# A recurrence and a two-layer network on one core: scans instead of triangle sums for four chunks, a third set of input buffers, a longer search for the order

## The chip, the cores and the metric

The kernel runs on one core of a Trainium2 chip. Its time is the device time of the whole program in microseconds (us); the figure for a kernel is the median of its runs. A core has TensorE (PE, matmuls), VectorE (DVE), ScalarE (ACT), GpSimd (POOL) and SyncE (SP), which issues the transfers here. Each engine works through its own list of instructions in order and waits on semaphores for the others.

## The reference

Two parts follow each other. The first is a gated recurrence over 768 time steps for each of 4 batches and 8 heads, with a 48 by 48 state; the second is a two-layer network over all 3072 tokens.

```python
f = 1.0 / (1.0 + np.exp(-f_logit))                 # (4, 8, 768, 48)
for t in range(S):
    state = f[:, :, t, :, None] * state + np.einsum('bhd,bhe->bhde', k[:, :, t], v[:, :, t])
    y[:, :, t] = np.einsum('bhd,bhde->bhe', q[:, :, t], state)
x = y.transpose(0, 2, 1, 3).reshape(B * S, H * D)  # 3072 tokens x 384
h = x @ w_in                                       # 384 -> 2048
sp = np.where(h > 20.0, h, np.log1p(np.exp(np.minimum(h, 20.0))))
g = h * np.tanh(sp)
out = g @ w_out                                    # 2048 -> 384
```

All is float32, and the result has to be close to it, which is why each matrix operand of the network is split into a high and a low part and three products are taken of each pair.

## The kernel before

**The recurrence** is cut into 24 chunks: 6 stretches of 128 steps for each of 4 batches, in the order stretch, then batch. Heads are worked on in pairs, four pairs to a chunk. A chunk goes through these steps. `load` brings the gate logits l, k, q (128 x 512 each) and v. `prep` takes the logarithm of the gate (ACT) and sums it along the chunk: for the first `NS` = 8 chunks by matmuls with an upper triangle (PE, line 362; these chunks are loaded transposed, as `ft`), for the others by a scan on DVE (line 367). Two exponentials of the sums (ACT) scale k and q; for chunks 1 to 7 k is scaled on POOL, else on DVE. `attn0` multiplies q and k in halves of 64 steps (scores, line 398) and masks them (DVE). `attn1` transposes k (line 423, copied by ACT to kt). `attn2` forms the state's update (line 440), sums it in mid and tmp (DVE, for the first four chunks partly ACT). `attn3` adds up the outputs (lines 474 and 486), decays the state (POOL), and writes the high and low parts of the outputs into xt; after a few chunks three transfers of SP rearrange rows of xt (line 525, the swap).

**The network** works on groups of 512 tokens (four chunks), 6 groups, and 16 tiles of the hidden width: 96 units. A unit is nine matmuls for the hidden tile (`moe_in`, line 219), a chain of nine steps for the activation (`mish`, lines 229 to 237: ACT, ACT, DVE, DVE, ACT, ACT, DVE, ACT, POOL), and, two units later, nine matmuls into the three output banks (`moe_out`, line 242). Groups 0 and 1 take turns with the first eight and the last eight tiles, so the weights are needed little by little. Each of the 16 weight tiles is loaded as 64-bit numbers (line 320) and split into high and low parts by `split_w` (two ACT and four DVE instructions, lines 322 to 330).

**The order.** No loop issues an instruction directly. Each step is recorded with its engine, an assumed cost and what it reads and writes; `Plan.order` then packs all steps in time by ranks, forwards and backwards, ten times for each of five settings, keeps the packing with the earliest end, and `issue` emits the steps in that order on every engine's list. `port` marks steps of DVE that must not overlap POOL in the plan. Where the plan leaves PE a gap before the first output of the network, `issue` puts in fillers, matmuls of zeros (`idle`, line 310):

```python
if self.start[i] <= self.start[self.until]:
    while at + 313.0 < self.start[i]:
        self.idle()
        at += 213.0 if at > 6500.0 else 426.0
```

The inputs l, k, q and v have two buffers each, so chunk n reuses those of chunk n - 2 (`i = n % 2`); kt, inv, mid and tmp have one each, and the two halves of the masked scores a one each.

**The end.** The fast path holds only where no decay has become too small. After all units DVE counts the chunks' final decays that are large enough, PE adds the counts, DVE writes the `flag` (lines 620 to 625); every engine loads it into a register (line 633), and where the count is short a general, slow path is run (line 634 on). With these inputs it is jumped over.

## Time and profile before

| | |
|---|---|
| median of 3 runs | 529.99 us (527.87 to 534.02) |
| profiled execution, its own time | 533.71 us |
| its span, first to last instruction | 531.9 us |
| mean granted TensorE clock | 0.990 of full speed |
| instructions | 13034 |
| idle fillers on PE | 66 matmuls, 132 records, 20.7 us busy |
| moved by DMA | 48.91 MB, 92 GB/s on average |

An instruction of PE appears as a weight load (PEld) and a matmul (PE); float32 matmuls have two records each. In rows of groups stand line, engine, operation, tiles and shapes, count, then busy us and mean ns of one, then the idle time of the engine just before them and what ended it. In the chain of waits each row has start, length, engine and line: followed back from the end, it names at each step what the step had waited for. An engine's name with a q (SPq, PEldq) is its sequencer: branches, semaphores, issues of transfers.

### The profile page before, as it was taken

The numbers are of one execution on the slowest core, as the hardware profiler recorded it, in microseconds if no ns is written. First come the engines' busy times: TensorE is split into PE (matmuls) and PEld (weight loads), VectorE is DVE, ScalarE is ACT, GpSimd is POOL, SyncE is SP. The second block draws the span as 40 slices with busy tenths as digits, with TensorE's granted clock in tenths as the row PEclk, the third lists the DMA queues.
The fourth block names the chain that finished last, engine by engine and source line by source line (L and its number), as shares of the span: only waits on it lengthen the run. The fifth ranks groups of instructions, "written<-read, shape, count | busy, mean of one in ns | idle before, by whom it ended". The sixth has DMA issues, their size and how long they took to land.

```text
span 531.9 us, 13034 instructions
## 1 busy us (share of the span) xinstructions
PE 512.8 (96%) x5358; PEld 409.7 (77%) x5358; DVE 369.7 (70%) x588; ACT 415.4 (78%) x731; POOL 157.4 (30%) x134
## 2 busy tenths in 40 slices
PE   8899999999899999999999999999999999999993
PEld 7678777777677777787787777787787787778882
DVE  4478999899897887866576777567657563645451
ACT  6777988888789798878778788878878776778770
POOL 2231442334132322412322332413131222132320
PEclk9899999999899999999999999999999999999998
DMA  7597554344230443321212330112221000000001
GB/s 263 208 293 257 167 173 131 88 154 140 98 99 21 143 138 110 118 64 60 62 41 90 101 100 25 58 41 90 61 79 41 4 0 33 26 33 1 1 1 67
DMA packets 22629, 48.91 MB, mean 92 GB/s; under 512 B 2656, under 2 KB 3808, under 8 KB 22560
## 3 DMA queue, kind: packets, MB, share of 16 engines
q1 hardware_dynamic: 22560, 47.98, 28.1%
q8 instruction: 44, 0.72, 0.6%
q14 instruction: 25, 0.20, 0.1%
HBM read 39.32 MB, written 6.29 MB: 86 GB/s over the span
## 4 chain that ended last, share of the span: by engine, by line
PE 82%; DVE 7%; DMA 3%; ACT 3%; issue 2%; SPq 0%; POOL 0%; DVEq 0%; ACTq 0%
PE h L219 35%; PE o L242 34%; PE at L486 2%; PE at L474 2%; PE at L440 2%; DMA xt<-xt 2%; PE at L423 2%; PE at L398 2%; DVE wt L325 1%; DMA raw<-ww 1%; DVE g L232 1%; DVE wl L330 1%; DVE n L231 1%; PE at L362 1%; PE o L310 1%
## 5 line engine op out<-in xcount | busy, mean ns | idle before, releaser
L237 POOL TENSOR_TENSOR gl<-g,gh 128x512 fp32r<-128x512 f32 x96 | 129.9, 1356 | 302.5 <-ACT gh L236 274.3
L219 PE MATMUL h<-xt,wh 128*128 128x512 f32 x576 | 185.9, 404 | 3.4 <-DVE g L235 2.4
L219 PEld LDWEIGHTS h<-xt,wh 128*128 128x128 f32 x576 | 105.7, 189 | 31.1 <-DVE g L235 4.8
L242 PE MATMUL o<-gh,wh 128*128 128x512 f32 x288 | 116.5, 405 | 0.0
L219 PE MATMUL h<-xt,wl 128*128 128x512 f32 x288 | 114.2, 397 | 0.0
L242 PE MATMUL o<-gl,wh 128*128 128x512 f32 x288 | 113.7, 395 | 0.0
L242 PE MATMUL o<-gh,wl 128*128 128x512 f32 x288 | 113.7, 395 | 0.0
L231 DVE SCALAR_TENSOR_TENSOR n<-n 128x512 f32<-128x512 f32 x96 | 71.1, 740 | 54.7 <-ACT n L230 54.5
L235 DVE TENSOR_TENSOR g<-g,h 128x512 f32<-128x512 f32 x96 | 65.3, 682 | 42.1 <-ACT h L234 41.7
L229 ACT ACTIVATE n<-h,hcap 128x512 f32<-128x512 f32 x96 | 65.7, 685 | 31.5 <-PE h L219 30.8
L233 ACT ACTIVATE h<-n,two 128x512 f32<-128x512 f32 x96 | 65.8, 686 | 29.3 <-DVE g L232 29.3
L236 ACT ACTIVATE gh<-g 128x512 fp32r<-128x512 f32 x96 | 60.1, 627 | 16.1 <-DVE g L235 14.1
L232 DVE TENSOR_TENSOR g<-h,n 128x512 f32<-128x512 f32 x96 | 66.1, 689 | 8.9 <-POOL gl L237 1.1
L230 ACT ACTIVATE n<-n,hcap 128x512 f32<-128x512 f32 x96 | 69.2, 721 | 2.1
L219 PEld LDWEIGHTS h<-xt,wl 128*128 128x128 f32 x288 | 54.4, 189 | 13.3
L242 PEld LDWEIGHTS o<-gh,wh 128*128 128x128 f32 x288 | 54.0, 188 | 13.5 <-ACT ob L588 0.3
L242 PEld LDWEIGHTS o<-gl,wh 128*128 128x128 f32 x288 | 54.0, 187 | 13.3
L242 PEld LDWEIGHTS o<-gh,wl 128*128 128x128 f32 x288 | 54.1, 188 | 11.8
L234 ACT ACTIVATE h<-h 128x512 f32<-128x512 f32 x96 | 55.9, 582 | 1.8
L519 DVE TENSOR_TENSOR xt<-at,xt 128x256 fp32r<-128x256 f32 x40 | 15.9, 418 | 13.4 <-ACT xt L512 13.2
L502 POOL TENSOR_TENSOR state<-tmp,ends 128x256 f32<-128x256 f32 x20 | 16.7, 834 | 28.6 <-PE at L474 22.1
L404 DVE TENSOR_TENSOR a<-at,causal 128x256 f32<-128x256 f32 x44 | 17.7, 418 | 7.4 <-PE at L398 7.3
(102 smaller groups left out, 525.2 us busy)
## 6 DMA issues: line engine op xcount, KB each, us to landing
raw<-ww SPq DMA_DIRECT2D x16, 768.0 KB, 5.2
v<-vn SPq DMA_DIRECT2D x24, 256.0 KB, 3.7
k<-kk SPq DMA_DIRECT2D x23, 256.0 KB, 3.1
q<-qq SPq DMA_DIRECT2D x23, 256.0 KB, 2.9
out<-ob SPq DMA_DIRECT2D x18, 256.0 KB, 2.3
l<-fl SPq DMA_DIRECT2D x16, 256.0 KB, 2.7
xt<-xt SPq DMA_DIRECT2D x15, 128.0 KB, 2.1
l<-ft SPq DMA_DIRECT2D x7, 256.0 KB, 3.8
```

The source lines that it names most:

```text
L219: nc.tensor.matmul(h, w[:, j, a * P : (a + 1) * P], xt[:, x, a, :], start=(n == 0), stop=(n == 3 * NK - 1))
L229: ("act", T_ACT(GT, True, 1), 0, lambda: nc.scalar.activation(u, h, AF.Relu, bias=hcap, scale=-1.0)),
L230: ("act", T_ACT(GT, False, 1), 0, lambda: nc.scalar.activation(u, u, AF.Exp, bias=hcap, scale=-1.0)),
L231: ("dve", T_DVE(GT), 1, lambda: nc.vector.scalar_tensor_tensor(n, u, 2.0, u, ALU.add, ALU.mult)),
L232: ("dve", T_DVE(GT), 0, lambda: nc.vector.tensor_tensor(g, h, n, ALU.mult)),
L233: ("act", T_ACT(GT, False, 1), 0, lambda: nc.scalar.activation(h, n, AF.Ln, bias=two)),
L234: ("act", T_ACT(GT, True), 0, lambda: nc.scalar.activation(h, h, AF.Exp, scale=-1.0)),
L235: ("dve", T_DVE(GT), 0, lambda: nc.vector.tensor_tensor(g, g, h, ALU.mult)),
L236: ("act", T_ACT(GT), 0, lambda: nc.scalar.activation(gh, g, AF.Copy)),
L237: ("pool", T_POOL(GT), 1, lambda: nc.gpsimd.tensor_tensor(gl, g, gh.bitcast(F32), ALU.subtract)),
L242: nc.tensor.matmul(o, w[:, j, m * P : (m + 1) * P], x, start=(first and i == 0), stop=(last and i == 2))
L404: add("dve", T_DVE(NP * CH), lambda e=e: nc.vector.tensor_tensor(a_[e], sc[e], causal[:, None, :].broadcast_to([P, NP, CH]), ALU.mult), [k ...
```

## The change

Seven edits are made together.

- `NS` is 4 instead of 8: chunks 4 to 7 are summed by scans on DVE from an untransposed load, as the later ones were. Their k stays on POOL, and inv in SBUF (`n < 2 * GC`).
- l, k, q and v have three buffers each (`NR`), kt, inv, mid and tmp two, a four.
- `Plan.order` goes on for 100 trials: the best ranks so far are disturbed by random amounts and packed again.
- A filler has 256 columns, and is put in where the plan's gap is over 527 ns.
- The count of the decays is recorded before the last two units' outputs, and DVE's last copies of outputs also wait for the flag.
- In the general path loops take the place of unrolled code, and some transfers go to ACT's queue.
- The program is built with 256 bytes of scratch for dynamic transfers.

```diff
-NS = 8
+NS = 4
...
+TRIALS = 100
+NR = 3
...
-                if best is None or end < best:
-                    best, self.start = end, start
+                if best is None or end < best[0]:
+                    best = end, rank, ahead, haste
+                    self.start = start
                 back = self.pack([-start[i] - cost[i] for i in range(count)], ahead, haste, True)
                 rank = [-back[i] - cost[i] for i in range(count)]
...
+        pick = random.Random(1)
+        for k in range(TRIALS):
+            end0, rank0, ahead, haste = best
+            spread = (200.0, 600.0, 2000.0, 6000.0)[k % 4]
+            rank = [r + pick.gauss(0.0, spread) for r in rank0]
+            start = self.pack(rank, ahead, haste)
+            end = max(start[i] + cost[i] for i in range(count))
+            if end < end0:
+                best = end, rank, ahead, haste
+                self.start = start
...
-                    while at + 313.0 < self.start[i]:
+                    while at + 527.0 < self.start[i]:
                         self.idle()
-                        at += 213.0 if at > 6500.0 else 426.0
+                        at += 427.0 if at > 6500.0 else 853.0
...
-        l_, k_, q_ = (ring(nm, 2, [P, NP, C]) for nm in "lkq")
-        v_ = ring("v", 2, [P, H * 64])
-        (kt_s,), (go,), (cum_,), (inv_s,) = (ring(nm, 1, [P, NP, C]) for nm in ("kt", "go", "cum", "inv"))
-        a_ = ring("a", 2, [P, NP, CH])
-        (mid,), (tmp,) = (ring(nm, 1, [P, NP, 64]) for nm in ("mid", "tmp"))
+        l_, k_, q_ = (ring(nm, NR, [P, NP, C]) for nm in "lkq")
+        v_ = ring("v", NR, [P, H * 64])
+        (go,), (cum_,) = (ring(nm, 1, [P, NP, C]) for nm in ("go", "cum"))
+        kt_, inv_ = (ring(nm, 2, [P, NP, C]) for nm in ("kt", "inv"))
+        a_ = ring("a", 4, [P, NP, CH])
+        mid_, tmp_ = (ring(nm, 2, [P, NP, 64]) for nm in ("mid", "tmp"))
...
-            nc.tensor.matmul(zeros[:, 0:P], state0[:, 0:P], state0[:, 0:P], start=True, stop=True)
+            nc.tensor.matmul(zeros[:, : 2 * P], state0[:, 0:P], state0, start=True, stop=True)
...
-            i = n % 2
+            i = n % NR
...
                 if n < NS:
-                    add("pe", 230 * st + 100, lambda s0=s0, dec=dec: [
+                    add("pe", 155 * st + 100, lambda s0=s0, dec=dec: [
...
-                if n < NS:
-                    inv, ki = inv_s[:, s], pairs("inv", ps)
+                if n < 2 * GC:
+                    inv, ki = inv_[n % 2][:, s], pairs(("inv", n % 2), ps)
                 else:
                     inv, ki = b[1].rearrange("p (a c) -> p a c", a=NP), [keys[1]]
                 add("act", T_ACT(w, n < NS), lambda cum=cum, inv=inv: nc.scalar.activation(inv, cum, AF.Exp), kc, ki)
                 add("act", T_ACT(w, n < NS), lambda cum=cum, dec=dec: nc.scalar.activation(dec, cum, AF.Exp, scale=-1.0), kc, kd)
-                times(0 < n < NS, w, k[:, s], k[:, s], inv, ki, kk_, port=n < NS)
+                times(0 < n < 2 * GC, w, k[:, s], k[:, s], inv, ki, kk_, port=n < 2 * GC)
...
-                        a_[e], sc[e], causal[:, None, :].broadcast_to([P, NP, CH]), ALU.mult), [keys[e]], [("a", e)])
+                        a_[2 * (n % 2) + e], sc[e], causal[:, None, :].broadcast_to([P, NP, CH]), ALU.mult), [keys[e]], [("a", n % 2, e)])
...
-            add("pe", 400, transposes, pairs(("k", n % 2)), [key])
-            add("act", T_ACT(GT, True), lambda: nc.scalar.activation(kt_s, b, AF.Copy), [key], ["kt"])
...
+            (mid, mk), (tmp, tk) = ((r[n % 2], (nm, n % 2)) for nm, r in (("mid", mid_), ("tmp", tmp_)))
...
-                add("pe", 1208, lambda: [update(), scores()], ["kt", ("v", n % 2)] + reads,
+                add("pe", 1208, lambda: [update(), scores()], [("kt", n % 2), ("v", n % NR)] + reads,
...
+            mid, tmp, a_x = mid_[n % 2], tmp_[n % 2], a_[2 * (n % 2) :]
...
-                pairs(("q", i)) + [("st", batch), "mid", ("v", i), ("a", 0), ("a", 1)], keys)
+                pairs(("q", i)) + [("st", batch), ("mid", n % 2), ("v", i), ("a", n % 2, 0), ("a", n % 2, 1)], keys)
...
+        def check():
+            ok, oks = at1[0:1, 0:1], state.rearrange("p b a c -> p (b a c)")[:, : NCH * NP]
+            add("dve", 119, lambda: nc.vector.tensor_scalar(
+                oks, ends.rearrange("p n a b -> p (n a b)"), DEC_OK, None, ALU.is_ge),
+                [x for n in range(NCH) for x in pairs(("end", n))], [("st", b) for b in range(B)])
+            add("dve", 169, lambda: nc.vector.tensor_reduce(okc, oks, mybir.AxisListType.X, ALU.add), [("st", 0)], ["okc"])
+            add("pe", 26, lambda: nc.tensor.matmul(ok, ones, okc, start=True, stop=True), ["okc"], [("at", 2)])
+            add("dve", 65, lambda: nc.vector.tensor_copy(flag, ok), [("at", 2)], ["flag"])
...
+
+                        add("dve", T_DVE(GT), lambda m=m: nc.vector.tensor_copy(ob_[m], o_[m]),
+                            [("o", m)] + ["flag"] * (u == len(units) - 1), pairs(("ob", m)))
...
+            if u == len(units):
+                check()
             if u >= LAG:
                 out_unit(u - LAG)
-
...
-                for p in range(NP):
+                with tc.For_i(0, NP, 1) as p:
...
-                        nc.sync.dma_start(
-                            dst, src.rearrange("(c b) p a t -> p a c b t", b=B)[:, p, :, ds(b, 1), :]
-                            .rearrange("p c b t -> p c (b t)"),
+                        nc.scalar.dma_start(
+                            dst, src.rearrange("(c b) p a t -> p a c b t", b=B)[:, ds(p, 1), :, ds(b, 1), :]
+                            .rearrange("p a c b t -> p (a c) (b t)"),
...
             with tc.For_i(0, NG, 1) as g:
...
-                for a in range(NK):
-                    for e in range(2):
-                        r, hd = 64 * e, head_at(a, e)
-                        for m in range(3):
-                            nc.sync.dma_start(
-                                x[r + m : r + 64 : 4, a, :], xs[hd * D + m : (hd + 1) * D : 3, tok]
-                            )
-                        r0 = head_at(NP - 1, e) * D
-                        nc.sync.dma_start(x[r + 3 : r + 64 : 4, a, :], xs[r0 + a : r0 + D : 3, tok])
+                rows = xs.rearrange("(a e r m) t -> a e m r t", e=2, r=D // 3, m=3)
+                for e in range(2):
+                    for m in range(4):
+                        src = rows[:NK, e, m, :, tok] if m < 3 else rows[NP - 1, e, :, :, tok]
+                        nc.scalar.dma_start(x[64 * e + m : 64 * e + 64 : 4], src.rearrange("a r t -> r a t"))
...
-                for j in range(NF):
-                    moe_in(h, xt, j)
-                    for *_, step in mish(h, n, g, gh, gl):
+                wj = [pool.tile([P, 1, W_TILE], F32R, tag=nm, name=nm) for nm in ("swh", "swl")]
+                total_o = st([P, NK, GT], "so")
+                nc.vector.memset(total_o, 0.0)
+                with tc.For_i(0, NF, 1) as j:
+                    for w, whole in zip(wj, (wh, wl)):
+                        nc.vector.tensor_copy(w, whole[:, ds(j, 1), :].bitcast(F32))
+                    moe_in(h, xt, 0, *(w[:, :, : NK * P] for w in wj))
+                    for *_, step in mish(h, n, g_, gh, gl):
                         step()
                     for m in range(NK):
-                        moe_out(o[m], m, gh, gl, j, j == 0, j == NF - 1)
-                for m in range(NK):
-                    nc.vector.tensor_copy(g, o[m])
-                    nc.sync.dma_start(out[m * P : (m + 1) * P, tok], g)
+                        moe_out(o[m], m, gh, gl, 0, True, True, *(w[:, :, NK * P :] for w in wj))
+                        nc.vector.tensor_tensor(total_o[:, m], total_o[:, m], o[m], ALU.add)
+                nc.sync.dma_start(out.rearrange("(m p) t -> p m t", p=P)[:, :, tok], total_o)
 
...
-    nc = bacc.Bacc("TRN2", target_bir_lowering=False, num_devices=1)
+    nc = bacc.Bacc("TRN2", target_bir_lowering=False, num_devices=1, dynamic_dma_scratch_size=256)
```

How the lists of the engines change at three places follows. The rows are the program's order on one engine, without times; line numbers after the change are 15 higher in `moe_in` and `mish` (L219 is L234, L231 is L246), 16 higher in `split_w`, `load` and `prep` (L320 is L336, L339 is L355, L367 is L383), and 18 higher at the swap (L525 is L543).

On SP, the end of the head in the program before: the last loads and weight tiles (raw) ahead of the first swap of rows in xt (L525) and up to the second; l_81, l_82 and so on are the two buffers of each input, the numbers the program's own.

```order
L339 DMA k_83<-kk 128x512
L339 DMA q_85<-qq 128x512
L342 DMA v_87<-vn 128x512
L339 DMA k_84<-kk 128x512
L525 DMA xt_97<-xt_97 32x2x384
L320 DMA raw_113<-ww 128x1536
L525 DMA xt_97<-xt_97 32x2x384 x2
L339 DMA q_86<-qq 128x512
L342 DMA v_88<-vn 128x512
L525 DMA xt_97<-xt_97 32x2x128
```

The same place after:

```order
L355 DMA k_86<-kk 128x512
L336 DMA raw_123<-ww 128x1536
L355 DMA k_84<-kk 128x512
L355 DMA q_89<-qq 128x512
L358 DMA v_92<-vn 128x512
L355 DMA q_87<-qq 128x512
L543 DMA xt_107<-xt_107 32x2x384
L336 DMA raw_122<-ww 128x1536
L543 DMA xt_107<-xt_107 32x2x384 x2
L543 DMA xt_107<-xt_107 32x2x128 x3
```

Before, 22 loads of an input (halves counted together) and 3 weight tiles stand ahead of the first swap, after it 28 and 4; the buffers l_83, k_86, q_89 and v_92 are the third ones, and inputs of chunks 6 and 7 have moved ahead of the swap.

On DVE, around the first unit's first instruction (L231 before, L246 after), before: L325 to L330 split weights, L357 bounds the gate, L519 forms the low part of xt, L277 scales q.

```order
L357 TENSOR_SCALAR l_81<-l_81 128x512
L325 SCALAR_TENSOR_TENSOR wt_114<-raw_112,wt_114 128x768
L330 TENSOR_TENSOR wl<-wt_115,wh 128x768
L327 SCALAR_TENSOR_TENSOR wt_114<-raw_112,wt_114 128x768
L519 TENSOR_TENSOR xt_98<-at_116,xt_98 128x2x128
L519 TENSOR_TENSOR xt_98<-at_117,xt_98 128x2x128
L231 SCALAR_TENSOR_TENSOR n_99<-n_99 128x512
L324 TENSOR_SCALAR wt_115<-wt_115 128x768
L232 TENSOR_TENSOR g_101<-h_119,n_99 128x512
L330 TENSOR_TENSOR wl<-wt_114,wh 128x768
L325 SCALAR_TENSOR_TENSOR wt_115<-raw_113,wt_115 128x768
```

After:

```order
L346 TENSOR_TENSOR wl<-wt_124,wh 128x768
L537 TENSOR_TENSOR xt_108<-at_126,xt_108 128x2x128
L346 TENSOR_TENSOR wl<-wt_125,wh 128x768
L340 TENSOR_SCALAR wt_124<-wt_124 128x768
L537 TENSOR_TENSOR xt_108<-at_127,xt_108 128x2x128
L293 TENSOR_TENSOR q_89<-q_89,at_126 128x512
L341 SCALAR_TENSOR_TENSOR wt_124<-raw_122,wt_124 128x768
L383 SCALAR_TENSOR_TENSOR cum_94<-go_93,l_81 128x512
L246 SCALAR_TENSOR_TENSOR n_109<-n_109 128x512
L343 SCALAR_TENSOR_TENSOR wt_124<-raw_122,wt_124 128x768
L247 TENSOR_TENSOR g_111<-h_129,n_109 128x512
```

After, a scan (L383, from l_81, chunk 6's gate) stands just ahead of L246; the scans of chunks 4 and 5 stand further ahead of it, that of chunk 7 behind the third L246. Before, the first scan on DVE is chunk 8's.

On SP, the end of the fast path, before: the last group's stores of outputs, the load of the flag and the branch past the general path.

```order
L592 DMA out<-ob_109 128x512
L592 DMA out<-ob_110 128x512
L592 DMA out<-ob_111 128x512
L633 TENSOR_LOAD flag
L633 ISA x2
L634 COMPARE_AND_BRANCH
```

After:

```order
L621 DMA out<-ob_119 128x512
L621 DMA out<-ob_120 128x512
L621 DMA out<-ob_121 128x512
L656 TENSOR_LOAD flag
L656 ISA x2
L621 DMA out<-ob_119 128x512
L621 DMA out<-ob_120 128x512
L621 DMA out<-ob_121 128x512
L657 COMPARE_AND_BRANCH
```

The load of the flag and the two instructions that check it have moved ahead of the last three stores; the branch follows the last store. From the branch to the place where the fast path goes on, the lists hold 147 rows before on SP, 307 on PE, 170 on ACT, 107 on DVE and 46 on POOL; after, 40, 54, 75, 51 and 40.

More of the change, by code (lines that the diff above doesn't have):

```diff
@@ L1 @@
+import random
 from contextlib import ExitStack
@@ L238, in mish, with moe_out @@
         )
-    def moe_out(o, m, gh, gl, j, first, last):
+    def moe_out(o, m, gh, gl, j, first, last, woh=woh, wol=wol):
         for i, (w, x) in enumerate(((woh, gh), (wol, gh), (woh, gl))):
@@ L440, in update @@
                             nc.tensor.matmul(
-                                u[c][half(e), p, :], kt_s[half(c), p, half(e)], v[half(c), c0 : c0 + 64], start=True, stop=True
+                                u[c][half(e), p, :], kt_[n % 2][half(c), p, half(e)], v[half(c), c0 : c0 + 64], start=True, stop=True
                             )
@@ L450, in attn2 @@
             else:
-                add("pe", 745, update, ["kt", ("v", n % 2)], keys[: 2 - last])
+                add("pe", 745, update, [("kt", n % 2), ("v", n % NR)], keys[: 2 - last])
             if n < B:
                 add("act", T_ACT(NP * 64, True), lambda: nc.scalar.activation(mid, u[0], AF.Copy),
-                    keys[:1], ["mid"])
+                    keys[:1], [mk])
             else:
-                add("dve", 337, lambda: nc.vector.tensor_tensor(mid, st, u[0], ALU.add), keys[:1] + [ks], ["mid"])
+                add("dve", 337, lambda: nc.vector.tensor_tensor(mid, st, u[0], ALU.add), keys[:1] + [ks], [mk])
             if not last:
-                add("dve", 337, lambda: nc.vector.tensor_tensor(tmp, u[1], mid, ALU.add), keys[1:] + ["mid"], ["tmp"])
+                add("dve", 337, lambda: nc.vector.tensor_tensor(tmp, u[1], mid, ALU.add), keys[1:] + [mk], [tk])
         def attn3(n):
-            i = n % 2
+            i = n % NR
             q, v = q_[i], v_[i]
             first, batch = n < B, n % B
+            mid, tmp, a_x = mid_[n % 2], tmp_[n % 2], a_[2 * (n % 2) :]
             b, keys = banks()
@@ L502, in attn3 @@
                 add("pool", T_POOL(NP * 64), lambda: nc.gpsimd.tensor_tensor(state[:, batch], tmp, decay, ALU.mult),
-                    pairs(("end", n)) + ["tmp"], [("st", batch)])
+                    pairs(("end", n)) + [("tmp", n % 2)], [("st", batch)])
             g, c = divmod(n, GC)
@@ L615, in recurrence_moe_kernel @@
                 attend()
+            if u == len(units):
+                check()
             if u >= LAG:
                 out_unit(u - LAG)
-        ok, oks = at1[0:1, 0:1], state.rearrange("p b a c -> p (b a c)")[:, : NCH * NP]
-        add("dve", 119, lambda: nc.vector.tensor_scalar(
-            oks, ends.rearrange("p n a b -> p (n a b)"), DEC_OK, None, ALU.is_ge),
-            [x for n in range(NCH) for x in pairs(("end", n))], [("st", b) for b in range(B)])
-        add("dve", 169, lambda: nc.vector.tensor_reduce(okc, oks, mybir.AxisListType.X, ALU.add), [("st", 0)], ["okc"])
-        add("pe", 26, lambda: nc.tensor.matmul(ok, ones, okc, start=True, stop=True), ["okc"], [("at", 2)])
-        add("dve", 65, lambda: nc.vector.tensor_copy(flag, ok), [("at", 2)], ["flag"])
         plan.idle = idle
@@ L674, in recurrence_moe_kernel @@
                             nc.scalar.activation(y[:, s], ps, AF.Copy)
-                        for i in range(2):
-                            nc.sync.dma_start(
-                                xs.rearrange("d (c b t) -> d c b t", b=B, t=C)[ds(e + (2 * p + i) * D, 1), :, ds(b, 1), :]
-                                .rearrange("d c b t -> d (c b) t"),
-                                y[i : i + 1, :].rearrange("d (c t) -> d c t", c=NCB),
-                            )
+                        nc.sync.dma_start(
+                            xs.rearrange("(i p d) (c b t) -> i p d c b t", i=2, d=D, b=B, t=C)[
+                                :, ds(p, 1), ds(e, 1), :, ds(b, 1), :
+                            ].rearrange("i p d c b t -> (i p d b) c t"),
+                            y.rearrange("i (c t) -> i c t", c=NCB),
+                        )
             with tc.For_i(0, NG, 1) as g:
```

28 lines of the change are left out of this document (14 added, 14 removed).

## The prediction

> **What bounds the kernel now.** I read the page, then a table of stages, then the chain of waits, then the last ten microseconds line by line.
>
> ```profile
> span 531.9 us, 13034 instructions
> PE 512.8 (96%) x5358; PEld 409.7 (77%) x5358; DVE 369.7 (70%) x588; ACT 415.4 (78%) x731; POOL 157.4 (30%) x134
> ```
>
> TensorE is busy 96% of the span, but the stages differ. Here is the table of busy time by stage; after the stage come its length and, for each engine, busy us and instructions, then the granted clock, the DMA share and GB/s.
>
> ```profile
> 0.00:10.00 10.00, 8.40 (x48) 7.94 (x52) 3.33 (x10) 6.72 (x17) 1.20 (x11) 1.00 0.74 237
> 10.00:20.00 10.00, 7.07 (x212) 6.00 (x208) 3.68 (x10) 6.66 (x15) 1.88 (x2) 0.95 0.79 290
> 20.00:44.40 24.40, 22.40 (x493) 19.42 (x491) 18.93 (x30) 17.72 (x39) 6.79 (x6) 0.95 0.74 238
> 44.40:160.00 115.60, 112.03 (x1108) 88.56 (x1109) 107.13 (x152) 98.30 (x165) 39.91 (x28) 0.99 0.44 142
> 160.00:522.70 362.70, 362.70 (x3509) 287.74 (x3507) 235.88 (x386) 286.05 (x499) 107.59 (x87) 1.00 0.18 56
> 522.70:531.90 9.20, 0.15 (x3) 0.05 (x2) 0.74 (x2) 0.00 (x0) 0.00 (x0) 0.77 0.27 96
> ```
>
> The columns are PE, PEld, DVE, ACT, POOL. The head (to 44.4) is four chunks of attention on cold buffers; DVE is busy 3.33 + 3.68 + 18.93 = 25.9 of 44.4 us. From 160 on PE has no gap, so whatever PE work is left there is the time. Behind the last matmul stand 9.2 us in which nothing computes. The middle is settled by DVE: 107.13 of 115.6 us. Its groups there, costliest first, with count, busy us and mean ns:
>
> ```profile
> L231 DVE SCALAR_TENSOR_TENSOR n<-n 128x512 f32<-128x512 f32 x22 | 17.4, 790 | 1.1 <-ACT n L230 1.0
> L330 DVE TENSOR_TENSOR wl<-wt,wh 128x768 fp32r<-128x768 f32 x13 | 16.7, 1281 | 0.4 <-ACT wh L329 0.4
> L325 DVE SCALAR_TENSOR_TENSOR wt<-raw,wt 128x768 int32<-128x768 int32 x12 | 13.9, 1162 | 0.0
> L327 DVE SCALAR_TENSOR_TENSOR wt<-raw,wt 128x768 int32<-128x768 int32 x12 | 13.7, 1138 | 0.0
> ```
>
> So by 160 us DVE has served 22 of the 96 units (22 times L231) and split the weights. The chain of waits runs through it, and PE waits at its end (chain, then PE's row in the timeline, then the stage behind it):
>
> ```profile
> 131.65 1.96 DVE wl L330
> 133.61 0.87 DVE wt L325
> 134.48 0.61 DVE g L235
> 135.13 3.88 PE h L219 x9
> 135.13 1.22 PE L219 MATMUL h<-xt,wh 128*128 128x512 f32 x2 [2.13 <-DVE g L235]
> 136.00:138.00 2.00, 2.00 (x6) 1.52 (x6) 2.00 (x3) 1.20 (x2) 1.17 (x1) 0.50 0.00 0
> ```
>
> The head ends on a transfer, the swap of the fourth chunk's rows in xt (chain of waits):
>
> ```profile
> 15.52 2.57 issue
> 38.44 5.91 DMA xt<-xt
> 44.39 2.37 PE h L219 x9
> ```
>
> **The change, part by part.** The sum is made against the profiled execution, span 531.9 us and time 533.71 (1.8 us lie around the span). It is a late one: the median of the runs is 529.99, so 3.7 us are taken off at the end.
>
> *Triangle sums for chunks 4 to 7.* Rows of the chain and of the groups:
>
> ```profile
> 23.97 0.91 PE at L362 x8
> L367 DVE TENSOR_TENSOR_SCAN cum<-go,l 128x512 f32<-128x512 f32 x16 | 22.7, 1416 | 0.0
> ```
>
> One chunk's four triangle matmuls (eight records) hold PE 0.91 us; four chunks 3.6 us. They stand in the last part of the head and the first of the middle, where DVE is the bound, so removing them is worth 0 and 3.6 us only if DVE isn't late. In exchange DVE gets four scans of 1.416 us, 5.7 us, in the engine that decides. In the new order three of the four stand ahead of the first L231 (L246 after), in the head, where DVE idles 44.4 - 25.9 = 18.5 us; they cost 3 x 1.416 = 4.2 us if that cover is gone. The fourth stands in the saturated middle: +1.4 us. From the 22nd unit's first layer on, both orders hold the same groups of PE work, and PE has no gap there; so the body moves by what the 22nd unit moves. I take +1.4; ends -3.6 (PE's saving counts in full, the scans lie in gaps) and +5.7 (no scan is hidden).
>
> *Third input buffers, two of kt, inv, mid, tmp and a.* They let a chunk's loads and products start before the chunk two ahead has left. In the head that puts more transfers ahead of the swap: 28 loads and 4 raw weight tiles instead of 22 and 3, by the order. With their sizes
>
> ```profile
> raw<-ww SPq DMA_DIRECT2D x16, 768.0 KB, 5.2
> k<-kk SPq DMA_DIRECT2D x23, 256.0 KB, 3.1
> ```
>
> this is 6 x 256 + 768 = 2304 KB, or 2.36 MB, at the 290 GB/s of 10 to 20 us some 8.1 us of transfer; ahead of the last swap it is 3 x 256 KB, 2.7 us. What hides it is that loads start earlier (the stage 20 to 44.4 moves only 238 GB/s). Taken: 0, since the new order also puts all of chunk 4's products ahead of the first unit; ends -2.6 (the 2.57 us stall at 15.52 goes) and +8.1.
>
> *The search and the fillers.* The longer search is that order. Fillers are 66 of 128 columns before, 32 of 256 after. From the timeline
>
> ```profile
> 37.31 3.07 PE L310 MATMUL o<-state 128*128 128x128 f32 x26
> ```
>
> 13 of them (two records each) take 3.07 us, 0.236 each, so 15.6 us before and, at twice the columns, 32 x 0.472 = 15.1 after. They stand in gaps: 0, at worst one of 0.47 us in the way.
>
> *The end.* The flag is now made before the last units' outputs, SP loads it ahead of its last three stores, and the general path is shorter. Rows of the timeline and the DMA table, of the lines that load the flag, branch and close the program (counts, shortest, median and longest ns, first and last start), and of the queues that bring instructions (count, MB):
>
> ```profile
> 522.09 1.74 SPq L592 DMA_DIRECT2D out<-ob  x3
> out<-ob SPq DMA_DIRECT2D x3, 256.0 KB, 2.1
> L633 PEldq TENSOR_LOAD <-flag x1: 767/767/767, 523.6 to 523.6; - x1
> L634 POOLq COMPARE_BRANCH  x1: 45/45/45, 524.4 to 524.4; - x1
> L634 POOLq EVENT_SEMAPHORE  x1: 17/17/17, 524.9 to 524.9; - x1
> L634 PEldq COMPARE_BRANCH  x1: 3542/3542/3542, 524.4 to 524.4; - x1
> L634 SPq COMPARE_BRANCH  x1: 50/50/50, 524.7 to 524.7; - x1
> L634 SPq EVENT_SEMAPHORE  x8: 17/17/17, 528.6 to 529.1; - x8
> L773 SPq EVENT_SEMAPHORE  x10: 17/28/28, 529.2 to 531.8; - x10
> L773 SPq DRAIN  x3: 7/7/7, 531.0 to 531.4; - x3
> q8 instruction: 44, 0.72, 0.6%
> q14 instruction: 25, 0.20, 0.1%
> ```
>
> POOL jumps over the general path in 0.5 us (524.4 to 524.9), over 46 rows of the order; SP jumps over 147 and needs 3.9 us (524.7 to 528.6), PE over 307 and 3.5. After, the jumps are PE 54, DVE 51, ACT 75, POOL and SP 40 rows. So SP's and PE's stall should go, and SP leaves its last store at 522.09 + 1.74 = 523.8 with the branch next, 0.9 us sooner than 524.7. What is late then: that store lands 2.1 us after its issue, near 526, and the closing of the program, from SP's first drain at 531.0 to the last semaphore at 531.8 0.8 us, brings the end to about 526.8: 531.9 - 526.8 = -5.1, say -5.0 us. If ACT or PE still pays 3.5 us behind a flag load of 0.77, the end is 522.7 + 0.8 + 3.5 + 0.8 = 527.8, with the drain between some 528.1: -3.8. If all still pay, -0.9. Taken, between the first two, since POOL's row is the nearest for SP (40 rows) and only ACT (75) lies far from it: -4.4. The check adds waits: its matmul stands on PE with the last outputs queued behind it, and DVE's last copies stand behind the flag; its inputs are a reduction of values long there, so 0, at worst one DVE instruction of 0.8 us (790 ns above). The shorter general path, its queue and the smaller scratch are not run otherwise: 0.
>
> [...]
>
> Sum: +1.4 + 0 + 0 - 4.4 = -3.0 us: span 528.9, own time 530.7, median 529.99 - 3.0 = 527.0.
>
> **The rivals.** 1, *faster*: the reordered middle uses DVE better. For it: DVE is idle 115.6 - 107.13 = 8.5 us there, and the split's last step, 1.96 us in the chain, took half of that in the head:
>
> ```profile
> 37.73 0.96 DVE L330 TENSOR_TENSOR wl<-wt,wh 128x768 fp32r<-128x768 f32 x1 [0.91 <-ACT wh L329]
> ```
>
> Against: the old order was packed by the same rules, and DVE's waits in the groups above are a few us at most. Half the idle time is 4.2: +1.4 - 4.2 - 4.4 = -7.2, 522.8.
>
> 2, *slower than before*: the loads running ahead hold the swap back. Place: xt's swap behind the weight tiles in the head. It decides once the first unit starts more than 3.0 us later than 44.4, at 47.4. For it: DMA is at 0.74 to 0.79 share throughout the head, and the swap took 5.91 us behind other transfers. Between 2.7 and 8.1, 5.4: +1.4 + 5.4 - 4.4 = +2.4, 532.4; at 8.1, 535.1.
>
> 3, *the end doesn't shrink*: the branch targets still have to be fetched, the jumps of 51 to 75 rows being longer than POOL's 46. +1.4 - 0.9 = +0.5, 530.5.
>
> 4, *PE, lightened, loses its clock*: a wait of 2.13 us for DVE was followed by a granted clock of 0.50 and a nine-matmul group of 3.88 us, where a later one (chain of waits) takes 2.10, 1.8 less.
>
> ```profile
> 303.15 2.10 PE h L219 x9
> ```
>
> With 3.6 us less work PE waits more; two more such waits cost 3.6: +1.4 + 3.6 - 4.4 = +0.6, 530.6. [...]
>
> **How the numbers follow.** Forecast 0.36 (its own range, body -1.2, if the stall at 15.52 goes as well, to +3.0 and end -5.0 to -3.8, is 523.8 to 529.2); rival 1 0.28, 2 0.15, 3 0.12, 4 0.09. The likeliest gives 527.0. The range 521.5 to 532.5 takes in rival 1 with 1.3 us beyond it and rival 2 at its middle. One per cent, 5.3 us, is about what a measurement of this kernel tells from no change, its runs lying 527.87 to 534.02. Faster by more is below 524.7: nine tenths of rival 1 (0.25) and a fifth of the forecast (0.07), with 0.01 of the others 0.33. Slower by more is above 535.3, which rival 2 reaches only at its far end: a third of it, 0.05, and 0.02 of the others, 0.07. Within: 0.60.
>
> **What would show it.** The stage behind the last matmul falls from 9.2 us to about 4.8, SP's semaphores following its branch within a microsecond: else rival 3. The first L234 matmul (L219 now) starts at 44 to 46; after 47.4 it is rival 2. The 22nd L246 ends near 161; before 158 it is rival 1. No PE group of 3.8 us more than now between 45 and 160: else rival 4. Were PE to show gaps behind the 22nd unit, the step that carries the body's shift to the end would be wrong.

## The result, and the profile after

The changed kernel takes 523.86 us (median of 521.81 to 525.3) against 531.11 us before (527.87 to 534.02, four runs each): ratio 0.985, 95% interval 0.981 to 0.989. Faster by 1.5%, inside the predicted range, but 3 us beyond the predicted 527.0: what came is rival 1, which had named 522.8. Beside the later experiments the same kernel gave 522.65 us and 0.981 (0.977 to 0.986).

The profiled execution of after has a span of 520.0 us and its own time is 521.81, so it is an early one, as before's (533.71) is a late one; of the 11.9 us between the spans, 2 to 5 are luck of these two runs (the medians differ by 7.3 us here and by 9.6 in the later set). From the page of after:

```profile
span 520.0 us, 12828 instructions
PE 506.1 (97%) x5258; PEld 399.3 (77%) x5258; DVE 370.4 (71%) x592; ACT 415.1 (80%) x731; POOL 155.1 (30%) x134
```

To compare stages I cut both spans at the same events: the first matmul of the first unit's first layer, the end of the 22nd and of the last `n` on DVE (L231 before, L246 after). Columns as in the prediction's stage table. Before, from the middle on:

```profile
44.39:160.61 116.22, 112.65 (x1111) 89.09 (x1112) 107.74 (x152) 98.92 (x166) 40.04 (x29) 0.99 0.43 142
160.61:514.43 353.82, 353.82 (x3471) 280.84 (x3470) 232.60 (x381) 281.94 (x493) 104.86 (x85) 1.00 0.19 58
514.43:531.85 17.42, 8.42 (x38) 6.43 (x36) 3.42 (x7) 3.50 (x6) 2.60 (x2) 0.88 0.14 51
```

After, with the second part of the head, and as a last row the stage behind the last matmul (9.20 before):

```profile
20.00:42.78 22.78, 21.34 (x530) 16.27 (x529) 20.77 (x31) 20.30 (x44) 9.44 (x8) 1.00 0.74 248
42.78:152.02 109.24, 106.74 (x987) 83.10 (x986) 105.91 (x153) 95.03 (x158) 35.89 (x27) 1.00 0.46 152
152.02:505.77 353.75, 353.59 (x3470) 280.67 (x3469) 230.60 (x383) 282.63 (x494) 104.01 (x85) 1.00 0.18 55
505.77:520.03 14.26, 8.30 (x36) 6.34 (x34) 3.35 (x5) 3.49 (x6) 2.59 (x2) 0.96 0.17 60
514.07:520.03 5.96, 0.00 (x0) 0.00 (x0) 0.69 (x1) 0.00 (x0) 0.00 (x0) 0.91 0.38 139
```

The head gives 1.6 us, the middle 7.0, the body nothing (353.82 and 353.75), the end 3.2. In the middle DVE idles 116.22 - 107.74 = 8.5 us before and 3.3 after: 5.2 of the 7.0. The other 1.8 us are busy time: three scans stand there instead of one (4.7 us for 2.0), but other instructions are shorter or fewer, `n` above all (15.8 us for 17.4, rows in the prediction and below). The head's 1.6 is luck: in two experiments with before's order it took 42.5 and 42.6 us, and in the second profile of after 45.0. Their middles, 115.0 and 115.7 us, put the middle's gain at 6 to 7.

Where DVE's idle time went is seen chunk by chunk. First rows of before, from the timeline: the outputs of a chunk on TensorE (`a,v`, L486), DVE's last copies of them out of their banks (L519), then the triangle sum of the next chunk (`tri`, L362). Then from after: the scan on DVE that replaces that sum (L383), and the outputs of the chunk ahead of it (L504).

```profile
47.20 0.80 PE L486 MATMUL at<-a,v 64*64 64x64 f32 x48
48.54 0.76 DVE L519 TENSOR_TENSOR xt<-at,xt 128x256 fp32r<-128x256 f32 x2 [0.51 <-ACT xt L512]
50.12 1.05 PE L362 MATMUL at<-tri,l 128*128 128x128 f32 x8
59.56 0.80 PE L486 MATMUL at<-a,v 64*64 64x64 f32 x48
60.90 0.76 DVE L519 TENSOR_TENSOR xt<-at,xt 128x256 fp32r<-128x256 f32 x2 [0.82 <-ACT xt L512]
62.49 1.05 PE L362 MATMUL at<-tri,l 128*128 128x128 f32 x8
```
```profile
36.73 1.22 DVE L383 TENSOR_TENSOR_SCAN cum<-go,l 128x512 f32<-128x512 f32 x1
41.16 0.83 PE L504 MATMUL at<-a,v 64*64 64x64 f32 x47
46.66 1.22 DVE L383 TENSOR_TENSOR_SCAN cum<-go,l 128x512 f32<-128x512 f32 x1
51.79 0.83 PE L504 MATMUL at<-a,v 64*64 64x64 f32 x47
```

Before, the sum of chunk 5 starts 2.1 us behind the end of chunk 4's outputs (50.12 against 48.00), that of chunk 6 at 62.49 behind 60.36, each 0.8 us behind the end of the copies: one chunk begins where the other ends. After, the scan of chunk 5 stands 5.3 us ahead of the end of chunk 4's outputs (36.73 against 41.99), that of chunk 6 6.0 us ahead (46.66 against 52.62). Chunk 4's outputs end 6 us sooner (41.99 against 48.00). What follows the sum moves with it: POOL scales k of chunks 5 and 6 from 52.35 and 64.46 before, 4.1 to 4.4 us behind the last chunk's outputs, and from 39.17 and 53.00 after, 2.8 us ahead of them and 0.4 behind. The code says why this can be: from chunk 4 on, the steps that take a pair of PSUM banks (where the kernel's matmuls write) with `banks()` have one pair, the outputs of a chunk use it too, and the triangle sum is written into it; the scan is written to `cum` in SBUF, and a bank is wanted only when the decay is made from it.

The end, in the rows of the line that branches over the general path (count, shortest, median and longest ns, first and last start); after:

```profile
L657 SPq EVENT_SEMAPHORE  x8: 17/17/17, 518.1 to 518.7; - x8
L657 PEldq COMPARE_BRANCH  x1: 358/358/358, 511.9 to 511.9; - x1
L657 ACTq COMPARE_BRANCH  x1: 50/50/50, 513.9 to 513.9; - x1
L657 ACTq EVENT_SEMAPHORE  x1: 17/17/17, 514.4 to 514.4; - x1
L657 DVEq COMPARE_BRANCH  x1: 72/72/72, 515.0 to 515.0; - x1
L657 SPq COMPARE_BRANCH  x1: 50/50/50, 515.2 to 515.2; - x1
L657 DVEq EVENT_SEMAPHORE  x1: 21/21/21, 518.5 to 518.5; - x1
```

PE (3.5 us before, now 0.4) and ACT (0.5 us from branch to semaphore) no longer stall. SP still does, 515.2 to 518.1, and DVE, 515.0 to 518.5. DVE jumps over 51 rows and stalls, ACT over 75 and doesn't: rows jumped aren't what decides.

### The profile page after: what moved, and what is told of

It is laid out like the page before. It is cut to its first block, busy times and chain, and to the rows that moved or that the text cites. A ratio compares the mean times of both kernels' runs of the same rounds, so it can differ in the third digit from the quotient of the medians.

```text
span 520.0 us, 12828 instructions
## 1 busy us (share of the span) xinstructions
PE 506.1 (97%) x5258; PEld 399.3 (77%) x5258; DVE 370.4 (71%) x592; ACT 415.1 (80%) x731; POOL 155.1 (30%) x134
## 4 chain that ended last, share of the span: by engine, by line
PE 73%; DVE 11%; ACT 8%; issue 3%; DMA 3%; SPq 1%; DVEq 0%; ACTq 0%
PE h L234 32%; PE o L257 32%; DVE g L250 2%; PE at L457 2%; PE at L504 2%; PE at L492 2%; DVE n L246 2%; DVE g L247 2%; DVE wt L341 2%; DMA l<-ft 1%; PE at L414 1%; PE at L439 1%; DMA raw<-ww 1%; ACT h L248 1%; ACT n L244 1%
## 5 line engine op out<-in xcount | busy, mean ns | idle before, releaser
L252 POOL TENSOR_TENSOR gl<-g,gh 128x512 fp32r<-128x512 f32 x96 | 128.2, 1336 | 294.3 <-ACT gh L251 262.7
L234 PE MATMUL h<-xt,wh 128*128 128x512 f32 x576 | 185.0, 402 | 1.6 <-DVE g L250 1.5
L234 PEld LDWEIGHTS h<-xt,wh 128*128 128x128 f32 x576 | 104.9, 188 | 29.2 <-DVE g L250 4.7
L234 PE MATMUL h<-xt,wl 128*128 128x512 f32 x288 | 113.7, 395 | 0.0
L246 DVE SCALAR_TENSOR_TENSOR n<-n 128x512 f32<-128x512 f32 x96 | 67.1, 699 | 59.8 <-ACT n L245 59.7
L234 PEld LDWEIGHTS h<-xt,wl 128*128 128x128 f32 x288 | 54.0, 187 | 13.2
L383 DVE TENSOR_TENSOR_SCAN cum<-go,l 128x512 f32<-128x512 f32 x20 | 26.7, 1334 | 0.0
L520 POOL TENSOR_TENSOR state<-tmp,ends 128x256 f32<-128x256 f32 x20 | 16.7, 835 | 21.6 <-PE at L492 17.4
```

The source lines that it names most:

```text
L234: nc.tensor.matmul(h, w[:, j, a * P : (a + 1) * P], xt[:, x, a, :], start=(n == 0), stop=(n == 3 * NK - 1))
L246: ("dve", T_DVE(GT), 1, lambda: nc.vector.scalar_tensor_tensor(n, u, 2.0, u, ALU.add, ALU.mult)),
L252: ("pool", T_POOL(GT), 1, lambda: nc.gpsimd.tensor_tensor(gl, g, gh.bitcast(F32), ALU.subtract)),
L383: add("dve", 2 * T_DVE(w) - 70, lambda s=s, cum=cum: nc.vector.tensor_tensor_scan(cum.rearrange("p a c -> p (a c)"), go[:, s].rearrange("p ...
```

## The experiments

### Only the end: the short general path alone, the early flag alone

```
(before) with tc.If(good < total):   -> the short general path of after
(before) check() at the program's end -> ahead of the last units' outputs, as in after
```

> The kernel before with only the short general path; same order of work, flag still made and loaded at the end. Both traces so far: behind the last matmul 9.2 us before and 5.9 after; SP's stall behind its branch 3.9 and 2.9 us, and before a second SP stall of 1.3. [...] So the stage behind the last matmul falls from 9.2 to about 6.9 (the second stall and 1.0 of the first go), the time by 2.3 us, ratio 0.996. The prediction's reading (rows jumped): SP's and PE's stall goes altogether, stage about 5.5, ratio 0.993. Rival (the early flag makes all of the end's gain): stage 9.2, ratio 1.000.

> The kernel before with only the early flag: check ahead of the last outputs, SP's load ahead of the last stores; jumps as long as before. Theory: SP's branch comes 0.9 us sooner behind the last matmul (1.1 instead of 2.0, as after has it), and all jump stalls stay: stage behind the last matmul 8.3, time -0.9 us, ratio 0.998. With the short path's -2.3 this makes up the 3.3 us of the two traces. Rival (the parts don't add, the flag is what the end waits for): stage about 6, ratio 0.994.

Measured: 0.998 (0.994 to 1.002) and 0.999 (0.996 to 1.002). The stage behind the last matmul, of the kernel with the short path and then of the one with the early flag:

```profile
519.78:526.71 6.93, 0.12 (x3) 0.02 (x2) 0.74 (x2) 0.00 (x0) 0.00 (x0) 0.84 0.33 121
```
```profile
520.51:527.91 7.40, 0.00 (x0) 0.00 (x0) 0.69 (x1) 0.00 (x0) 0.00 (x0) 0.66 0.32 116
```

The short path takes 2.3 us from the 9.2, as expected: SP still stands 3.0 us at its branch (521.8 to 524.8) and DVE 3.3, ACT 0.4 and PE 0.3. The early flag takes 1.8, between theory and rival. After's end is 3.2 us shorter, less than the two added, so by these single traces they overlap by 0.9. Times this close to before's can't show more than that neither is worth 1%: the rest of the gain isn't at the end.

### Without the search, with later branches

```
-TRIALS = 100
+TRIALS = 0
```
```
+    spare = ctile([1, 1], F32, "spare")
 (check)  nc.vector.tensor_copy(flag, ok), then 30 times nc.vector.memset(spare, 0.0)
 (stores of groups 2 to 4)  one DMA of 512 columns -> four of 128
```

In the trace of after the 8 KB packets of instructions come when DVE has run 64, 191, 320, 448 and 576 instructions (37.70 to 325.58 us), 127 to 129 apart, and SP 81 and 208; the trace doesn't name a packet's engine. A block, below, is such a stretch of 128 instructions. The position theory is the author's estimate from the jumps of before and after (ACT without a stall over 75 rows, DVE with one over 51): a branch stalls or not by the blocks in which it and its target stand, not by the rows jumped. How an engine holds its instructions no trace shows.

> The kernel after without the hundred random trials of the order; triangle sums, buffers, fillers and end as after. After is 8 us (1.5%) under before, 3.3 of it at the end; the rest is the middle, where DVE idles 3.3 us instead of 8.5, and the head. Theory 1 (the search closes DVE's gaps): without it only the end and little else is left, ratio 0.992 to 0.994, DVE idle 7 us or more between the first unit's first layer and the end of the 22nd L246. Theory 2 (the buffers and the moved sums do): ratio 0.985 to 0.987, DVE idle 3 to 4 us there. [...]

> The kernel after, same order, with instructions added late so that SP's and DVE's branches stand elsewhere in their block: 30 one-element memsets on DVE behind the flag, and the nine stores of output groups 2 to 4 cut in four each on SP (27 more DMAs). [...] Position theory: no stall on any engine; SP then waits for the last store, 2.1 to 2.6 us behind its issue, and the stage behind the last matmul falls from 5.9 to about 4.2; 1.7 us under after, ratio to before about 0.982 beside after's 0.985. Rival (length of the jump, or something else at the branch): stalls of 2.9 (SP) and 3.4 us (DVE) as in after, stage 5.9, ratio 0.985 or a little over.

The kernel without the search gave 0.985 (0.978 to 0.991), the gain of after. Its middle, and its DVE at the end:

```profile
43.64:155.18 111.54, 107.74 (x985) 83.88 (x984) 106.55 (x153) 95.81 (x160) 35.20 (x27) 0.98 0.42 143
```
```profile
L657 DVEq COMPARE_BRANCH  x1: 72/72/72, 518.5 to 518.5; - x1
L657 DVEq EVENT_SEMAPHORE  x1: 21/21/21, 522.1 to 522.1; - x1
```

DVE idles 5.0 us, nearer to after's 3.3 than to 8.5, at a clock of 0.98. So the search is worth some 2 us in the middle, by one trace. DVE's stall stayed (3.6 us).

The kernel with later branches gave 0.974 (0.968 to 0.981) where 0.982 was expected, but not by the end. There DVE's stall is gone (0.6 us) and SP's is not (3.1), and the stage behind the last matmul is as long as in after (6.18 us for 5.96), so SP's stall by itself is enough to set it:

```profile
L660 SPq EVENT_SEMAPHORE  x8: 17/17/17, 517.3 to 517.8; - x8
L660 DVEq COMPARE_BRANCH  x1: 72/72/72, 514.0 to 514.0; - x1
L660 SPq COMPARE_BRANCH  x1: 50/50/50, 514.2 to 514.2; - x1
L660 DVEq EVENT_SEMAPHORE  x1: 21/21/21, 514.6 to 514.6; - x1
```

That both stalls would go rested on the author's estimate of one offset, 62, for all engines (what is added to an instruction's number to count its blocks of 128). Sorting the 8 KB instruction packets of the traces by how many instructions each engine had run when they came gives DVE 64, ACT about 62 and SP 48. With these offsets, found after the fact, the jumps of SP, DVE and ACT below sort by blocks: 2.6 to 3.6 us where the target lies two on, 0.5 and 0.6 where it lies one on (instruction of the branch and of its target, offset added, block of 128; time from the branch to the next instruction):

```
DVE after        828 ->  966   block 6 -> 8   3.5 us
DVE no search    823 ->  961   block 6 -> 8   3.6
DVE later        863 -> 1001   block 7 -> 8   0.6
ACT after        858 -> 1020   block 7 -> 8   0.5
ACT early flag   860 -> 1143   block 7 -> 9   2.6
SP  after        309 ->  487   block 2 -> 4   2.9
SP  later        336 ->  514   block 2 -> 4   3.1   (last instruction of its block)
```

What it gained lies in the body, 350.87 us for 353.75; the two last runs below take that up.

### The moved sums and the room

```
(eight sums)       NS = 4 -> 8
(two inputs)       NR = 3 -> 2
(all room back)    NR = 2; kt, inv, mid, tmp one each, a two
```

> The kernel after once more, as the yardstick for the three kernels beside it. Ratio to before 0.985 as found (0.981 to 0.989). From the first unit's first layer to the end of the 22nd L246: 109 us (before 116, and 115 to 116 in the two kernels with only the end changed).

> The kernel after with the triangle sums kept for eight chunks as before (chunks 4 to 7 by TensorE, not by DVE's scan); buffers, fillers, search and end as after. The search finds its own order for it. Rest of the gain is 5 to 6 us in the stretch from the first layer to the end of the 22nd multiply on DVE, and leaving out the search cost little of it (0.985 without). Theory S (the moved sums bring it: a chunk leaves its PSUM bank and PE sooner): the stretch is back at 114 to 116 us, ratio 0.994 to 0.996. Theory B (the buffers bring it): stretch 108 to 110, and as in the prediction's term DVE is a scan shorter there, -1.4: ratio 0.982 to 0.986.

> The kernel after with two input buffers (l, k, q, v) as before instead of three; kt, inv, mid, tmp and a keep their second set, all else as after. Theory B1 (the third input buffer brings the middle's gain, since a chunk's loads and its first exps no longer wait for the chunk two ahead): stretch 114 to 116 us, ratio 0.994 to 0.996. Theory B2 (the doubled products bring it): 109, ratio 0.984 to 0.987. By the prediction's own term (room is worth 0, at worst the loads hold the swap back) it would be the same or up to 2.7 us faster.

> The kernel after with all its new room taken back: two input buffers, one each of kt, inv, mid and tmp, two of a; sums on four chunks, search, fillers and end as after. Theory B (room is the cause): the stretch is back at 114 to 116 us and the ratio at 0.994 to 0.996, only the end's gain staying. Theory S (the moved sums): stretch 109, ratio 0.984 to 0.987. If both this and the kernel with sums on eight chunks keep the gain, each alone suffices; if both lose half, they add.

Ratios: after 0.981 (0.977 to 0.986), eight sums on TensorE 0.995 (0.992 to 0.998), two input buffers 0.983 (0.979 to 0.987), all room taken back 0.992 (0.989 to 0.995). The middle of each, in that order:

```profile
44.99:153.85 108.86, 106.80 (x987) 83.16 (x986) 105.77 (x153) 95.13 (x158) 35.72 (x27) 1.00 0.43 148
```
```profile
42.32:159.31 116.99, 112.22 (x1094) 87.19 (x1089) 109.37 (x159) 98.67 (x166) 38.53 (x29) 0.99 0.43 145
```
```profile
41.20:149.17 107.97, 105.49 (x992) 82.51 (x983) 103.62 (x150) 94.96 (x162) 35.81 (x28) 1.00 0.43 143
```
```profile
41.89:157.33 115.44, 108.49 (x1066) 83.33 (x1065) 111.32 (x152) 96.54 (x162) 43.91 (x29) 1.00 0.41 136
```

Theory S holds: with the sums back on TensorE, room, search and end as in after, the middle is 117 us, 8.1 more than after's 108.9 in the same set: DVE idles 7.6 us there (3.1 in after) and is busy 3.6 us more, `n` taking 803 ns for 708 and the first steps of one more weight tile's split standing there. The chunks wait for each other again (timeline of that kernel; the sum of chunk 5 starts 2.1 us behind the end of chunk 4's outputs, 48.06 against 45.93):

```profile
45.13 0.80 PE L504 MATMUL at<-a,v 64*64 64x64 f32 x48
48.06 1.05 PE L378 MATMUL at<-tri,l 128*128 128x128 f32 x8
```

The third input buffer is worth nothing (108 us without it). Without any of the room the middle is lost too, in another way: DVE idles little more (4.1 us) but is 5.5 us busier. `n` takes longer, and POOL's `gl` with it (groups of the middle, this kernel and then after):

```profile
L246 DVE SCALAR_TENSOR_TENSOR n<-n 128x512 f32<-128x512 f32 x22 | 18.0, 818 | 0.9 <-ACT n L245 0.9
L252 POOL TENSOR_TENSOR gl<-g,gh 128x512 fp32r<-128x512 f32 x21 | 35.9, 1713 | 61.2 <-ACT gh L251 61.1
```
```profile
L246 DVE SCALAR_TENSOR_TENSOR n<-n 128x512 f32<-128x512 f32 x22 | 15.8, 717 | 0.2 <-ACT n L245 0.2
L252 POOL TENSOR_TENSOR gl<-g,gh 128x512 fp32r<-128x512 f32 x21 | 30.2, 1439 | 57.9 <-ACT gh L251 51.0 <-PE o L257 5.9 <-PE at L504 1.0
```

So the sums and the doubled products both have to be there; neither adds its own half. That the products are at fault, and not the inputs, follows only from the run with two input buffers: they weren't taken back by themselves, which of them it is stays open, and so does what makes `n` and `gl` longer. Each of these kernels is also packed anew, so its one order is part of the result; of the full change two orders were run, with middles of 109 and 111.5 us, a spread below half of these losses. The fillers, the lower cost that the plan assumes for a triangle sum, and the scratch were never taken back alone.

### Is it TensorE's time, or DVE's?

```
(sums' size added)  attn1, chunks 4 to 7: four times matmul(at1, tri, tri) ahead of the transposes
(scan twice)        prep, chunks 4 to 7: the tensor_tensor_scan issued twice
```

> The kernel after, same order, with four matmuls of the triangle sums' size added for each of chunks 4 to 7 on TensorE, in the step of that chunk's transposes and into the same bank, where the transposes overwrite them: 0.91 us of PE a chunk by the chain's row, and no other engine reads them. Extra work, output unchanged. Prediction's step (DVE bounds the middle, so the removed triangle sums are worth 0): middle stays at 109, time as after, ratio 0.981 to 0.985. New theory (PE bounded the middle as well, busy 112.65 of 116.2 us before and 106.7 of 109.2 after): the three of four chunks whose transposes stand in the middle cost 2.7 us there, middle 111.5 to 112, and the fourth up to 0.9 in the head; ratio 0.987 to 0.991.

> The kernel after, same order, with the scan of chunks 4 to 7 issued twice on DVE, same result twice. Two scans stand in the head, two of the four in the middle. If the scans in the head lie in DVE's idle time and the middle is bounded by DVE (the prediction), the two in the middle cost 2 x 1.3 = 2.7 us, ratio 0.986 to 0.990, middle 111.5 to 112. If every scan counts: 4 x 1.33 = 5.3, ratio 0.992 to 0.995. If only PE bounds the middle: 0 to 1, middle 109 to 110, ratio 0.981 to 0.986. Together with the added triangle matmuls: both engines bound it if both cost their share.

Ratios 0.993 (0.990 to 0.995) and 0.991 (0.988 to 0.994). Their middles:

```profile
48.05:156.68 108.63, 107.74 (x1003) 84.95 (x1002) 104.95 (x151) 94.04 (x158) 35.29 (x27) 1.00 0.44 146
```
```profile
43.84:156.49 112.65, 108.19 (x987) 84.25 (x986) 108.40 (x155) 95.15 (x159) 35.42 (x27) 0.98 0.44 144
```

The "new theory" of the first expectation falls: the time of three chunks' sums costs TensorE nothing in the middle, 108.6 against 108.9 and 109.2, though TensorE is busy 97% of it. Two scans more cost 3.6 us there, a little over their 2.7, while the two in the head show no cost beyond the spread of its length (43.8, between after's 42.8 and 45.0). The middle is DVE's, as the prediction said. What the moved sums brought is therefore neither engine's time; what is left, and what the timelines show, is the place of the sum in the chain from chunk to chunk.

The added matmuls miss both expected ratios: they cost some 4 us in the head (48.05 us for 42.8 to 45.0), by a way nobody had named. From the timeline and a two-microsecond table of that run:

```profile
36.72 0.30 PE L507 MATMUL at<-a,v 64*32 64x64 f32 x2 [2.63 <-issue]
```
```profile
34.00:36.00 2.00, 0.09 (x12) 0.00 (x0) 1.74 (x3) 0.74 (x2) 0.25 (x1) 1.00 1.02 371
38.00:40.00 2.00, 1.92 (x5) 1.65 (x6) 1.02 (x2) 1.52 (x6) 0.00 (x0) 0.50 0.15 49
```

TensorE waits 2.63 us from 34.09 on for nothing that the profile shows ("issue") while the loads run at 371 GB/s, and from 38 to 40 computes at a granted clock of 0.50. What it waited for, and why the added matmuls bring this wait, was not shown.

### The address, and SP's branch

```
(moved by 32 bytes)  + spare = ctile([1, 1], F32, "spare")      and nothing else
(later still)        as the kernel with later branches, but 15 stores cut in four
```

> The kernel after with one unused one-element tile ahead of the working tiles, nothing else: it moves every tile behind it by 32 bytes, so that xt, gh and gl start at a multiple of 64 bytes (before and after they stand at 32 over one; also in the kernel with late additions they were moved so). In that kernel one matmul followed the next after 229 ns in the stretch 165 to 500 us, in all other kernels after 233. Theory (the address): 229 ns here too, from the end of the 22nd L246 to the last one 350.9 us instead of 353.8, ratio about 0.975. Rival (the cut stores or the additions did it): 233 ns, 353.8, ratio 0.981 to 0.985. The end as in after, 5.9 us behind the last matmul with both stalls.

> As the first kernel with late additions, but 15 stores cut in four instead of nine: SP jumps from instruction 352 to 530, DVE from 865 to 1003. In the first one DVE's stall went (0.6 us behind its branch) and SP's stayed (3.1). Sorting the fetches of 8 KB by the instructions that each engine had run puts SP's block ends at 80, 208 and 336 instructions and DVE's at 64, 192 and on by 128: so SP stood on the last instruction of a block there (336), with its target two blocks on, and here it stands 16 into the next, target one block on. Theory: SP's stall goes as well, its next instruction follows within 0.6 us, SP then waits for the last store, and the stage behind the last matmul falls from 5.9 to 4.2 us; 1.7 us under the kernel with only the moved addresses, ratio about 0.972. Rival (SP's wait is for something else): 3 us behind the branch, stage 5.9 to 6.2.

Ratios 0.977 (0.974 to 0.980) and 0.980 (0.977 to 0.983). The body of the first, and one of its groups of matmuls there; then the same group of after:

```profile
153.61:502.67 349.06, 348.77 (x3470) 280.96 (x3469) 230.14 (x382) 282.07 (x494) 104.11 (x85) 1.00 0.18 56
```
```profile
L258 PE MATMUL o<-gh,wl 128*128 128x512 f32 x217 | 84.6, 390 | 0.0
```
```profile
L257 PE MATMUL o<-gh,wl 128*128 128x512 f32 x217 | 85.7, 395 | 0.0
```

The address alone does it: one unused tile takes 4.7 us from the body, and in the trace one 512-column matmul follows the next after 229 ns instead of 233 (L235 from 45.64 to 49.07, 15 of them; in after L234 from 44.05 to 46.85, 12). The addresses are those of the built programs, and the tile moves all that stand behind it; which of them matters wasn't separated. This is the fastest kernel here, 518.34 us.

The other one shows SP without a stall (0.6 us from branch to semaphore; the rows are rounded) and an end of 5.2 us, at which SP now waits for its last stores; and it shows what the additions cost:

```profile
L660 SPq EVENT_SEMAPHORE  x8: 17/17/17, 513.0 to 515.0; - x8
L660 SPq COMPARE_BRANCH  x1: 50/50/50, 512.3 to 512.3; - x1
```
```profile
511.20:516.36 5.16, 0.00 (x0) 0.00 (x0) 0.69 (x1) 0.00 (x0) 0.00 (x0) 0.94 0.43 157
```
```profile
457.36 0.73 PE L235 MATMUL h<-xt,wh 128*128 128x512 f32 x2 [1.51 <-DVE g L251]
```

With SP's offset of 48 the target lies one block on (352 to 530, block 3 to 4), as in the jumps without a stall above. The gain, 0.8 us, is half of the 1.7 expected, since the last store lands 2.7 us behind the branch; and with the thirty memsets on DVE TensorE waited 1.5 us for `g` near 457 (1.8 in the body, 0.3 with the moved addresses alone). So the ratio is 0.980 instead of 0.972, slower than with the moved addresses alone. A kernel with the moved address and branches placed without that cost wasn't run.

## Why the prediction was right or wrong

The time lies in the range because the range reached to rival 1, not because the sum held: the middle was put at +1.4 us and gave -6 to -7, the end at -4.4 and gave -3.2. The likeliest place, within one per cent of before (chance 0.60), was missed; faster by more (below 524.7) had 0.33.

*The bound of the middle*: right. DVE settles it; added TensorE work cost 0 there, added scans their time.

*Triangle sums, worth 0, +1.4 for the scan in the middle*: this is the step that failed. "Removing them is worth 0" took the sums as TensorE time beside a busy DVE. Taken alone the time is worth 0, as the added matmuls show. But the sum is also a link that holds the next chunk back until the bank is free, and with it back on TensorE the middle is 8 us longer. The prediction quoted the sum out of the chain of waits and priced it by its 0.91 us; the timeline of before, with each sum some 2 us behind the last chunk's outputs, would have shown the link. The bank as the reason is read from the code and these times; no run gave the old sum a bank of its own. The price of the scans was short as well: the prediction drew the line at the first L246 and counted one of the four in the middle, but from the first unit's first layer on two of them stand there, and with chunk 8's they take 4.7 us for 2.0.

*Buffers, 0*: right for the input buffers (one order of each), and the loads running ahead held nothing back: rival 2's mark of 47.4 wasn't reached in after (42.8 and 45.0). Wrong for the doubled products, without which the middle loses what the sums gave (115.4, with the input buffers taken back too).

*Search and fillers, 0*: about right, 2 us in one trace and nothing in the ratio.

*The end, -4.4*: the mechanism right, the size off, -3.2. PE and ACT stopped stalling (0.4 and 0.5 us), SP and DVE did not (2.9 and 3.5); the prediction's middle case had named ACT or PE as the ones left. POOL's row as the nearest for SP misled: DVE stalled at 51 rows and ACT not at 75, the times in the table sort by block, and the 40 and 51 rows of the lists are 178 instructions on SP and 138 on DVE. This was rival 3 for two engines of four, and for the one that sets the end. Packets of 8 KB of instructions do start while SP stands at its branch, five of them before (524.7 to 528.6 us) and two after (515.2 to 518.1); that the stall waits for them was not shown.

*What moves the 22nd unit moves the end*: right, 353.82 and 353.75 us.

*Rival 1*: came, with 8.5 us of DVE's idle time falling to 3.3 where half had been named. What was held against it, that the old order was packed by the same rules and DVE's waits were few, had no force: with the sum off the bank the packer had a constraint less.

*Rival 4*: the middle of after has a clock of 1.00, so it lost none.

*The late profile, -3.7*: one to two microseconds too much, since before's median was 531.0 to 532.2 in the later sets.

## What to carry to other kernels

Price an operation that a change moves by what it holds as well as by what it lasts: if it writes to a buffer that the stage ahead still uses, look in the timeline how long after that stage's end it starts, since that wait is what goes. An idle share of a few per cent on the engine that binds a stage is worth a look at the chain that makes it, even when every single wait is small. After any edit that adds or resizes tiles, look at the addresses and at the spacing of the matmuls.

## What the hardware showed that was not expected

- The tiles that TensorE streams in the network (xt, gh, gl) stand at 32 bytes over a multiple of 64 in before and after. Moved by 32 bytes with all that is behind them, a 512-column matmul follows the last after 229 instead of 233 ns, through the whole body: 4.7 us, 0.9%.
- In the jumps of the table and of SP in the last run, the next instruction came 2.6 to 3.6 us behind a taken branch whose target lay two 128-instruction blocks on, and 0.5 to 0.6 us behind one whose target lay one on: DVE's 138 instructions (3.5 and 0.6 us) and SP's 178 (3.1 and 0.6) took the one or the other by where the branch stood. The blocks are the spacing of the 8 KB instruction packets in after (127 to 129 instructions on DVE); what makes the branch wait was not shown.
- Under loads of 371 GB/s TensorE stood 2.63 us for nothing that the profile shows, in the run with the added matmuls, and the granted clock was 0.50 from 38 to 40 us. What it waited for no run shows.
